# Pooled attention and a gated token MLP on one core: earlier weights, another opening order, the rank count out of PSUM, dense work on banks by turns

## The chip, the cores and the metric

The kernel runs on one core of a Trainium2 chip. Five engines run side by side, each with its own queue of instructions in order: TensorE (PE) multiplies matrices into the accumulation memory PSUM, VectorE (DVE) and ScalarE (ACT) work on SBUF and PSUM, GpSimd (POOL) on SBUF, and SyncE (SP) issues transfers to 16 DMA engines. The metric is the device time of one execution in microseconds (us), lower is better. Before the change the median of three runs is 292.88 us (292.44 to 293.79).

## The reference, cut to what matters

```python
# attention: batch 8, heads 8, sequence 576, head width 64, pool 8
k_p = k.reshape(B, H, 72, 8, D).mean(axis=3)
v_p = v.reshape(B, H, 72, 8, D).mean(axis=3)
scores = scale * q @ k_p.T                      # 576 x 72 for each head
attn = exp(scores - max); attn /= attn.sum() + 1e-9
x = concat_heads(attn @ v_p)                    # (8, 576, 512)
# mixture of depths: for each batch b
s = x[b] @ w_gate                               # 576 scores
top = the 128 largest of s
out[b] = x[b]
out[b, top] = x[b, top] + sigmoid(s[top]) * (relu(x[b, top] @ w1) @ w2)   # w1 512x1024, w2 1024x512
```

## The kernel before, in words

One path (`direct_path`) does all of it. A second, general path runs only if a flag at the end says that a softmax sum left the range for which the first path is made; it does not run here.

**Units of work.** The queries of a batch go in three thirds of 192 (`TS * TL`); `u` counts them over the batches, 0 to 23, so batch b begins at u = 3b. A chunk `a` is 128 query rows (two tiles of 64); chunk numbers run over pairs of batches, 36 in all, and a third completes one or two of them by turns (`chunks[u]`).

**Attention.** `pool_k` adds rows of keys, `k_trans` transposes and finishes them on DVE. `pool_v` adds eight rows of values into the tile `vp` (three additions), multiplies by the gate weights `wg`, and `gate_v` reduces that product, so that the gate score comes out of the same matmul as the attention (one more column, and one for the softmax sum, filled by `eights`). `q_trans(u)` transposes the queries on DVE. `scores(u)` writes four PSUM banks (bank 0 to 3) with 32 matmuls, and ACT takes the exponential from each bank into `et`. `attend(a)` multiplies `et` by `vp` into a double bank `pA` (two of these), and `norm(a)` divides on DVE and stores.

**Selection.** `score(b)` sums the gate scores over heads. `row_bcast(b)` spreads the 576 scores along the rows of banks 0 and 1 (five columns of 128) by PE transposes, and ACT copies them to the SBUF tile `sr`. `count(b)` compares the row with each column of scores by five DVE instructions of 128 to 640 values (each pair of columns is compared once, with a mask `before` for the diagonal), which leaves partial counts and the comparisons `ge`. `one_hot(b)` sums the comparisons the other way on PE, subtracts (`rank`) and compares with `slots`, `gather(b)` turns that into the list of tokens `idx` and fetches their rows with an indirect DMA from the output tensor, issued by POOL.

**Dense work.** `x_trans` transposes the fetched rows (PE, copied by ACT into `xg`), `hidden` computes the hidden layer in parts of 3, 3 and 2 blocks, with a relu on ACT after each, `finish` the second layer in parts of 176, 176 and 160 columns; ACT scales, POOL adds, and POOL scatters the rows.

**Order.** The order on every engine is written out by hand: `at(u, slot, job)` files a job into third u and slot 0 to 7, and the main loop runs slot 0, the first chunk's `attend` and `norm`, slot 1, `scores(u + 1)`, slot 2, the second chunk, `q_trans(u + 2)`, slots 3 to 7. With w = 3(b + 1), the selection of batch b lies in thirds w to w + 2 and its dense work in w + 3 to w + 5, beside the attention of the next two batches; so from u = 6 on there is dense work in every third. Jobs filed into the same slot run in the order in which the loop over batches files them. SP issues loads and stores in the same order, and a load waits there for its buffer.

Four banks are shared by all this (`bank(i, shape)`, one buffer each); the other four are the two `pA`. The next user of a bank waits until the last one is read:

```python
p = [bank(i, [128, 2, TS * TL]) for i in range(4)]      # scores
p = bank(i, [C, len(cs), C])                            # row_bcast, i = 0 and 1
p = bank(2, [C, NC])                                    # one_hot, and gather
p = bank(0, [128, DB, cap])                             # x_trans
at(w + 3, 3, hidden, b, 0, 0)                           # hidden: banks 0, 1, 0
at(w + 4, 5, finish, b, 0, 1)                           # finish: banks 1, 2, 3
```

Of the kernel before, what the change touches and what calls it, by code (L numbers as in the profile page):

```python
# [48 lines left out]
def direct_path(ctx, tc, q, k, v, moe_w_gate, moe_w1, moe_w2, moe_capacity, out, flag):  # L49
# [67 lines left out]
    for i, t in enumerate(vraws):  # L117
        (nc.vector, nc.gpsimd)[i % 2].memset(t, 0.0)

    def load_v(b, g):  # L120
# [15 lines left out]
    nc.scalar.dma_start(out=wg.rearrange("p h d -> p (h d)"),  # L136
                        in_=bass.AP(tensor=moe_w_gate.tensor, offset=moe_w_gate.offset, ap=[[0, 128], [1, DM]]))
# [10 lines left out]
    diff = counted("diff", [C, C], [[1, C]], 0, -1)  # L148
    part = counted("part", [C, 1], [[0, 1]], 0, 1)
    steps = counted("steps", [C, C // G - 1], [[-G, C // G - 1]], -G, 1)  # L150
    numbers = counted("numbers", [C, NC - 1], [[1, NC - 1]], 0, 0)
# [6 lines left out]
    for t in kts + vps:  # L158
        nc.gpsimd.memset(t, 0.0)

    slots = counted("slots", [C, NC, cap], [[C, NC], [1, cap]], 1 - NC * C, 1)

    before = const.tile([C, NC, C], FT)
    nc.gpsimd.memset(before[:, 0 : NC - 1, :], 1.0)
# [11 lines left out]
    def constants():  # L176
        nc.vector.tensor_scalar(ident, diff, 0.0, None, op0=OP.is_equal)
        nc.vector.tensor_scalar(before[:, NC - 1, :], diff, 0.0, None, op0=OP.is_lt)
        nc.vector.memset(ones, 1.0)
        nc.vector.memset(one32, 1.0)  # L180

        ge, q16, q4, lo, hi = (const.tile([C, n], FT, name=x) for x, n in (
            ("ge", C // G - 1), ("q16", 1), ("q4", 1), ("lo", 1), ("hi", 1)))
        nc.vector.tensor_scalar(ge, steps, 0.0, None, op0=OP.is_ge, op1=OP.add, accum_out=q16)
        nc.vector.tensor_scalar(q4, q16, 4.0, None, op0=OP.mult)
        nc.vector.scalar_tensor_tensor(hi, q16, -float(G), part, op0=OP.mult, op1=OP.add)
        nc.vector.tensor_scalar(hi, hi, float(TG), None, op0=OP.mult)
        for i, a in enumerate(auxb):
            nc.vector.tensor_scalar(a[:, 0 : NC - 1, 0], numbers, 0.0, hi, op0=OP.mult, op1=OP.add)
            nc.vector.tensor_copy(a[:, NC - 1, 0:1], hi)  # L190
            nc.vector.tensor_scalar(a[:, i : i + NC - 1, 1], numbers, q4, None, op0=OP.add)
            h = (NC - 1) * (1 - i)
            nc.vector.tensor_scalar(a[:, h, 1:2], q16, float(32 - 4 * i), None, op0=OP.add)
# [35 lines left out]
    def pool_v(b, g, eng):  # L229
        x = VR[b, g]  # L230
        VP[b] = vps[b % 2]
        h = slice(HG * g, HG * g + HG)
        eng.tensor_tensor(out=x[:, :, 0:4, :], in0=x[:, :, 0:4, :], in1=x[:, :, 4:8, :], op=OP.add)  # L233
        eng.tensor_tensor(out=x[:, :, 0:2, :], in0=x[:, :, 0:2, :], in1=x[:, :, 2:4, :], op=OP.add)  # L234
        eng.tensor_tensor(out=VP[b][:, h, 0:D], in0=x[:, :, 0, :], in1=x[:, :, 1, :], op=OP.add)  # L235

        eng.tensor_tensor(out=x[:, :, 2, :], in0=VP[b][:, h, 0:D], in1=wg[:, h, :], op=OP.mult)  # L237
# [45 lines left out]
    def attend(a):  # L283
        PA[a] = psum.tile([C, 2, 512], FT, name="pA")
        for h in range(H):
            g, n = divmod(h, HG)
            for t in range(2):
                u, i = divmod(2 * a + t, TS)
                nc.tensor.matmul(PA[a][TL * t : TL * t + TL, g, E * n : E * n + E],  # L289
                                 ET[u][h // 2][:, h % 2, TL * i : TL * i + TL], VP[u // NTH][:, h, :],  # L290
                                 start=True, stop=True)
# [71 lines left out]
    def row_bcast(b):  # L363
        SR[b] = work.tile([C, NC, C], FT, name="sr", bufs=1)
        for i, cs in enumerate((range(0, NC - 1), range(NC - 1, NC))):
            p = bank(i, [C, len(cs), C])
            for c in cs:
                nc.tensor.transpose(p[:, c - cs[0], :], scs[b % 2][:, c : c + 1].to_broadcast([C, C]), ident)  # L368
            nc.scalar.copy(out=SR[b][:, cs[0] : cs[-1] + 1, :], in_=p)  # L369

    def count(b):

        CN[b] = work.tile([C, NC], FT, name="cn")
        GE[b] = [work.tile([C, c + 1, C], BF, name=f"ge{c}", bufs=1) for c in range(NC)]
        for c in range(NC):
            nc.vector.scalar_tensor_tensor(GE[b][c], SR[b][:, 0 : c + 1, :], scs[b % 2][:, c : c + 1],  # L376
                                           before[:, NC - 1 - c : NC, :], op0=OP.is_ge, op1=OP.mult,
                                           accum_out=CN[b][:, c : c + 1])

    def one_hot(b):  # L380

        p = bank(2, [C, NC])
        for c in range(NC):
            for i in range(c, NC):
                nc.tensor.matmul(p[:, c : c + 1], GE[b][i][:, c, :], ones, start=(i == c), stop=(i == NC - 1))
        rank = work.tile([C, NC, 1], FT, name="rank")
        nc.vector.tensor_tensor(out=rank[:, :, 0], in0=CN[b], in1=p, op=OP.subtract)
        OH[b] = work.tile([C, NC, cap], BF, name="oh", bufs=1)
        nc.vector.tensor_tensor(out=OH[b], in0=slots, in1=rank.to_broadcast([C, NC, cap]), op=OP.is_equal)

    def gather(b):

        p = bank(2, [cap, 5])
# [21 lines left out]
    def x_trans(b):  # L415
        p = bank(0, [128, DB, cap])
# [47 lines left out]
    for b in range(B):  # L464
        w = NTH * (b + 1)
        if b % 2:
            at(w - 1, 7, score, b)
        else:
            at(w, 1, score, b)
        for n, f in enumerate((row_bcast, count, one_hot, gather, gate, x_trans)):  # L470
            du, slot = ((0, 1), (0, 2), (0, 6), (1, 4), (1, 6), (2, 5))[n] if b == B - 1 else (
                (0, 3), (0, 7), (1, 3), (1, 7), (2, 2), (2, 7))[n]
            at(w + du, slot, f, b)
        at(w + 3, 3, hidden, b, 0, 0)
        at(w + 3, 5, hidden, b, 1, 1)
        at(w + 4, 3, hidden, b, 2, 0)
        at(w + 4, 5, finish, b, 0, 1)
        at(w + 5, 5, finish, b, 1, 2)
        at(w + 5, 6, finish, b, 2, 3)
        if b + 1 < B:  # L480
            u = NTH * b
            at(u, 1, pool_k, b + 1, nc.gpsimd)
            at(u, 7, pool_v, b + 1, 0, nc.gpsimd)
            at(u + 1, 3, k_trans, b + 1)
            at(u + 1, 7, pool_v, b + 1, 1, nc.gpsimd)
            at(u + 2, 3, gate_v, b + 1, 0)
            at(u + 2, 7, gate_v, b + 1, 1)
        if b + 2 < B:
            at(u, 2, load_k, b + 2)
            at(u, 2, load_v, b + 2, 0)  # L490
            at(u + 1, 3, load_v, b + 2, 1)
            at(u + 1, 3, load_q, b + 2)
# [9 lines left out]
    at(2, 2, lambda: nc.sync.dma_start(out=w1, in_=moe_w1.rearrange("(a p) f -> p a f", p=128)))  # L502
    at(3, 3, lambda: nc.sync.dma_start(out=w2, in_=moe_w2.rearrange("(a p) n -> p a n", p=128)))
    constants()
    pool_k(0, nc.vector)
    pool_v(0, 0, nc.gpsimd)
# [5 lines left out]
    eights()  # L512
    gate_v(0, 0)
    pool_v(0, 1, nc.vector)
    gate_v(0, 1)

    for u in range(NU + 6):
        run(u, 0)
        mine = chunks.get(u, ())
        for a in mine[0:1]:  # L520
            attend(a)
            norm(a)
        run(u, 1)
        if 0 < u < NU - 1:
            scores(u + 1)
        run(u, 2)
        for a in mine[1:]:
            attend(a)
            norm(a)
# [371 lines left out]
```

## Time and profile before

| | us | share of the span |
|---|---|---|
| span of the profiled execution | 292.5 | |
| PE busy | 222.7 | 76% |
| PE weight loads busy | 205.6 | 70% |
| DVE busy | 147.9 | 51% |
| ACT busy | 72.9 | 25% |
| POOL busy | 156.9 | 54% |
| data moved | 46.94 MB | 161 GB/s in the mean |

A busy time is a sum over stages that have different limits, so the table alone doesn't say what bounds the kernel. The page's second part cuts the span into 40 slices of 7.3 us (digits are tenths of busy time, PEclk tenths of the full TensorE clock that was granted). The largest groups are the hidden layer (PE, line 430, 64.2 us), the second layer (line 442, 59.2 us with its two widths), the attention (line 289, 46.6 us) and the scores (line 277, 43.8 us); on DVE the count (line 376, 37.8 us) and the normalisation (line 306, 22.1 us); on POOL the value pooling (lines 233 to 237). A line such as "PE bank L430 <- ACT sr L369: 5.7, 7, 1.1" among the waits says that PE, at the instruction of line 430, waited for ACT's instruction of line 369, 5.7 us in total, 7 times, at most 1.1 us. In the timeline a line begins with start and length in us, then engine, line, operation, output and input; what stands in brackets at its end is the idle time of the engine ahead of it and what ended it.

### The profile page before, as it was taken

The page shows a single profiled execution, that of the slowest core. Times are in us where ns is not written, and L with a number is a line of the kernel's source. Part 1 is how long each engine was busy: PE and PEld are TensorE (multiplying, and loading weights), DVE is VectorE, ACT ScalarE, POOL GpSimd, SP SyncE. Part 2 cuts the span into 40 slices and gives each one's busy share as a digit, 9 for nine tenths or more (in the row PEclk, how much of TensorE's full clock was granted, in tenths as well). Part 3 has the DMA queues.
Part 4 walks back from the last instruction along what each step waited for, and adds up shares of the span by engine and source line. Part 5 has one row for each costly group of instructions (what it writes and reads, how often), then busy time and mean ns, then how long its engine had stood idle before and what let it go on. Part 6 is the DMA issues. An engine that isn't in the chain of part 4 may idle for free.

```text
span 292.5 us, 7287 instructions
## 1 busy us (share of the span) xinstructions
PE 222.7 (76%) x3050; PEld 205.6 (70%) x3050; DVE 147.9 (51%) x367; ACT 72.9 (25%) x178; POOL 156.9 (54%) x191
## 2 busy tenths in 40 slices
PE   0071777174889898997898989987989899899980
PEld 0061666063789797886797878876978789799980
DVE  7978758934247166816474358443862443331000
ACT  2040225020213232332232233213222321212110
POOL 9499608665910979088906693679348102413221
PEclk9996879576879999999999999999999999999996
DMA  7998899953932567215943691312122202401001
GB/s 227 355 343 325 269 360 406 333 213 95 351 126 74 186 217 260 63 57 154 346 157 115 211 318 54 94 31 81 20 64 99 74 17 61 142 0 38 38 0 47
DMA packets 13048, 46.94 MB, mean 161 GB/s; under 512 B 1104, under 2 KB 1104, under 8 KB 10960
## 3 DMA queue, kind: packets, MB, share of 16 engines
q1 hardware_dynamic: 11584, 41.95, 42.4%
q0 software_dynamic: 1280, 4.20, 4.6%
q8 instruction: 26, 0.43, 0.6%
q10 hardware_dynamic: 144, 0.26, 0.3%
q14 instruction: 14, 0.11, 0.1%
HBM read 34.87 MB, written 11.53 MB: 159 GB/s over the span
## 4 chain that ended last, share of the span: by engine, by line
PE 50%; POOL 17%; DVE 12%; issue 10%; ACT 4%; DMA 3%; POOLq 0%; ACTq 0%
PE bank L430 16%; PE bank L442 14%; PE bank L277 8%; PE pA L289 8%; POOL vraw L233 5%; DMA vraw<-in_v_dram 3%; DVE ge L376 3%; POOL vraw L234 3%; DVE qt L267 2%; ACT et L281 2%; POOL kraw L215 2%; POOL vp L235 2%; POOL vraw L237 1%; ACT sr L369 1%; PE bank L368 1%
## 5 line engine op out<-in xcount | busy, mean ns | idle before, releaser
L430 PE MATMUL bank<-xg,w 128*128 128x128 f32 x512 | 64.2, 284 | 9.4 <-ACT sr L369 5.7
L430 PEld LDWEIGHTS bank<-xg,w 128*128 128x128 f32 x512 | 60.4, 196 | 13.5 <-ACT sr L369 7.4
L442 PE MATMUL bank<-w,ht 128*128 128x176 f32 (+1 forms) x384 | 59.2, 311 | 5.0 <-ACT et L281 5.0
L281 ACT ACTIVATE et<-bank 128x384 f32<-128x384 f32 x96 | 39.3, 496 | 92.6 <-PE bank L277 92.6
L442 PEld LDWEIGHTS bank<-w,ht 128*128 128x128 f32 x384 | 55.8, 190 | 6.3 <-ACT et L281 6.2
L444 POOL TENSOR_TENSOR y<-y,xr 128x176 f32<-128x176 f32 (+1 forms) x24 | 13.0, 543 | 85.5 <-ACT y L443 84.7
L277 PE MATMUL bank<-qt,kt 32*128 32x192 f32 x768 | 43.8, 364 | 18.3 <-DVE qt L267 14.4
L289 PE MATMUL pA<-vp,et 128*64 128x66 f32 x1152 | 46.6, 234 | 12.4 <-DVE vp L241 12.0
L289 PEld LDWEIGHTS pA<-vp,et 128*64 128x64 f32 x1152 | 40.8, 146 | 18.8 <-DVE vp L241 7.2
L376 DVE SCALAR_TENSOR_TENSOR ge<-sr,sc,before 128x128 bf16<-128x128 f32 (+4 forms) x40 | 37.8, 1003 | 30.1 <-ACT sr L369 30.1
L277 PEld LDWEIGHTS bank<-qt,kt 32*128 32x128 f32 x768 | 35.9, 205 | 20.9 <-issue 17.6
L233 POOL TENSOR_TENSOR vraw<-vraw 128x1024 f32<-128x1024 f32 x15 | 35.9, 2394 | 4.4 <-DMA vraw<-in_v_dram 4.2
L267 DVE STREAM_TRANSPOSE qt<-qraw 128x512 f32<-128x512 f32 (+1 forms) x48 | 24.5, 551 | 0.0
L432 ACT ACTIVATE ht<-bank 128x384 f32<-128x384 f32 (+1 forms) x24 | 10.9, 455 | 52.1 <-PE bank L430 52.1
L298 DVE RECIPROCAL rzall<-pA 128x8 f32<-128x8 f32 x36 | 7.3, 203 | 30.6 <-PE pA L289 30.6
L306 DVE TENSOR_TENSOR xs<-pA,rzall 128x512 f32<-128x512 f32 x32 | 22.1, 692 | 1.1
L443 ACT ACTIVATE y<-bank,g 128x176 f32<-128x176 f32 (+1 forms) x24 | 9.7, 403 | 52.3 <-PE bank L442 52.3
L413 DVE RECIPROCAL g<-g 128x1 f32<-128x1 f32 x8 | 1.3, 164 | 41.0 <-POOL g L412 41.0
L234 POOL TENSOR_TENSOR vraw<-vraw 128x512 f32<-128x512 f32 x15 | 19.4, 1290 | 1.2
L215 POOL TENSOR_TENSOR kraw<-kraw 128x1152 f32<-128x1152 f32 x7 | 18.4, 2628 | 0.0
L235 POOL TENSOR_TENSOR vp<-vraw 128x256 f32<-128x256 f32 x15 | 11.5, 767 | 1.2
L237 POOL TENSOR_TENSOR vraw<-vp,wg 128x256 f32<-128x256 f32 x15 | 11.4, 759 | 1.2
(85 smaller groups left out, 167.0 us busy)
## 6 DMA issues: line engine op xcount, KB each, us to landing
kraw<-in_k_dram SPq DMA_DIRECT2D x8, 1152.0 KB
qraw<-in_q_dram SPq DMA_DIRECT2D x8, 1152.0 KB
vraw<-in_v_dram SPq DMA_DIRECT2D x16, 512.0 KB
out_dram<-xs SPq DMA_DIRECT2D x16, 512.0 KB
w<-in_moe_w_dram SPq DMA_DIRECT2D x2, 2048.0 KB
vraw<-in_v_dram SPq DMA_DIRECT2D x16, 64.0 KB
out_dram<-xh SPq DMA_DIRECT2D x8, 128.0 KB
wg<-in_moe_w_gate_dram ACTq DMA_DIRECT2D x1, 256.0 KB
```

The source lines that it names most:

```text
L215: eng.tensor_tensor(out=x[:, :, 0:2, :], in0=x[:, :, 0:2, :], in1=x[:, :, 2:4, :], op=OP.add)
L233: eng.tensor_tensor(out=x[:, :, 0:4, :], in0=x[:, :, 0:4, :], in1=x[:, :, 4:8, :], op=OP.add)
L234: eng.tensor_tensor(out=x[:, :, 0:2, :], in0=x[:, :, 0:2, :], in1=x[:, :, 2:4, :], op=OP.add)
L235: eng.tensor_tensor(out=VP[b][:, h, 0:D], in0=x[:, :, 0, :], in1=x[:, :, 1, :], op=OP.add)
L267: nc.vector.transpose(out=QT[u][:, :, n : n + m, :].rearrange("p j t c -> p t j c"), in_=x)
L277: nc.tensor.matmul(p[i][:, s, :], KT[b][r, j, s, :], QT[u][r, j, :, G * s : G * s + G], start=(j == 0), stop=(j == 1))
L281: nc.scalar.activation(ET[u][i], p[i], AF.Exp, scale=exp_scale)
L289: nc.tensor.matmul(PA[a][TL * t : TL * t + TL, g, E * n : E * n + E], ET[u][h // 2][:, h % 2, TL * i : TL * i + TL], VP[u // NTH][:, h, :] ...
L306: nc.vector.tensor_tensor(out=XS[a][:, 0 if XS.get(a - 1) is not XS[a] else 1, :].rearrange("p (g n d) -> p g n d", g=2, d=D), in0=o[:, :, ...
L376: nc.vector.scalar_tensor_tensor(GE[b][c], SR[b][:, 0 : c + 1, :], scs[b % 2][:, c : c + 1], before[:, NC - 1 - c : NC, :], op0=OP.is_ge, ...
L430: nc.tensor.matmul(p[:, n, :], w1[:, d, 128 * f : 128 * f + 128], XG[b][:, d, :], start=(d == 0), stop=(d == DB - 1))
L442: nc.tensor.matmul(p, HT[b][:, f, :], w2[:, f, c], start=(f == 0), stop=(f == FB - 1))
```

## The change

It has seven parts. (1) The load of the first weights goes from third 2 to third 0 and that of the second from 3 to 1, ahead of batch 2's data, whose loads are filed a third later; the gate weights are loaded by SP's queue. (2) At the start, two of the four value buffers are cleared later and by POOL alone, the constants of the selection move from the head of DVE's queue to slot 3 of third 0, and `eights` comes first. (3) Where DVE pools values (one half of batch 0), a single reduction takes the place of three additions, and POOL always multiplies by the gate weights. (4) `row_bcast` leaves the row in banks 0 and 1, and `count` reads it there; its fifth comparison is split, as the row lies in two banks. `one_hot` puts the rank into PSUM. (5) The dense jobs and the selection use other banks, given by the schedule. (6) In thirds with one chunk, half of its heads are attended ahead of the next scores and half behind them. (7) The slots change: POOL's pooling of values comes ahead of the gather, the row of scores ahead of the hidden layer, the gather ahead of finish.

```diff
     vraws = [const.tile([128, HG, POOLW, D], FT, name=f"vraw{i}") for i in range(4)]
-    for i, t in enumerate(vraws):
-        (nc.vector, nc.gpsimd)[i % 2].memset(t, 0.0)
+
+    nc.vector.memset(vraws[0], 0.0)
+    nc.gpsimd.memset(vraws[1], 0.0)
...
-    for t in kts + vps:
+    for t in kts + vps + vraws[2:]:
         nc.gpsimd.memset(t, 0.0)
...
+        if eng is nc.vector:
+            eng.tensor_reduce(out=VP[b][:, h, 0:D], in_=x.rearrange("p h t d -> p h d t"), axis=AX.X, op=OP.add)
+        else:
...
-        eng.tensor_tensor(out=x[:, :, 2, :], in0=VP[b][:, h, 0:D], in1=wg[:, h, :], op=OP.mult)
+        nc.gpsimd.tensor_tensor(out=x[:, :, 2, :], in0=VP[b][:, h, 0:D], in1=wg[:, h, :], op=OP.mult)
...
     def row_bcast(b):
-        SR[b] = work.tile([C, NC, C], FT, name="sr", bufs=1)
...
-            nc.scalar.copy(out=SR[b][:, cs[0] : cs[-1] + 1, :], in_=p)
+        SR[b] = [bank(0, [C, NC - 1, C]), bank(1, [C, 1, C])]
...
         for c in range(NC):
-            nc.vector.scalar_tensor_tensor(GE[b][c], SR[b][:, 0 : c + 1, :], scs[b % 2][:, c : c + 1],
-                                           before[:, NC - 1 - c : NC, :], op0=OP.is_ge, op1=OP.mult,
-                                           accum_out=CN[b][:, c : c + 1])
...
+            if c == NC - 1:
+                nc.vector.tensor_scalar(GE[b][c][:, 0:n, :], SR[b][0], s, None, op0=OP.is_ge, op1=OP.add,
+                                        accum_out=CN[b][:, NC : NC + 1])
+            x, y, m = ((GE[b][c], SR[b][0][:, 0:n, :], before[:, NC - 1 - n :, :]) if c < NC - 1 else
+                       (GE[b][c][:, c : c + 1, :], SR[b][1], before[:, NC - 2 : NC - 1, :]))
+            nc.vector.scalar_tensor_tensor(x, y, s, m, op0=OP.is_ge, op1=OP.mult, accum_out=CN[b][:, c : c + 1])
+        nc.vector.tensor_tensor(out=CN[b][:, NC - 1 : NC], in0=CN[b][:, NC - 1 : NC], in1=CN[b][:, NC : NC + 1], op=OP.add)
...
-        for n, f in enumerate((row_bcast, count, one_hot, gather, gate, x_trans)):
-            du, slot = ((0, 1), (0, 2), (0, 6), (1, 4), (1, 6), (2, 5))[n] if b == B - 1 else (
-                (0, 3), (0, 7), (1, 3), (1, 7), (2, 2), (2, 7))[n]
-            at(w + du, slot, f, b)
-        at(w + 3, 3, hidden, b, 0, 0)
-        at(w + 3, 5, hidden, b, 1, 1)
-        at(w + 4, 3, hidden, b, 2, 0)
-        at(w + 4, 5, finish, b, 0, 1)
-        at(w + 5, 5, finish, b, 1, 2)
-        at(w + 5, 6, finish, b, 2, 3)
+        last = b == B - 1
+
+        at(*((w - 1, 3) if b % 2 else (w, 1)), score, b)
+        at(w, 1 if last else 3, row_bcast, b)
+        at(w, 1 if last else 3, count, b)
+        at(*((w, 7) if last else (w + 1, 3)), one_hot, b, 0)
+        at(w + 1, 5, gather, b, 3)
+        at(w + 2, 5, gate, b)
+        at(w + 2, 5, x_trans, b, 2)
+        at(w + 3, 4, hidden, b, 0, 2)
+        at(w + 3, 6, hidden, b, 1, 3)
+        at(w + 4, 4, hidden, b, 2, 1)
+        at(w + 4, 6, finish, b, 0, 2)
+        at(w + 5, 4, finish, b, 1, 0)
+        at(w + 5, 6, finish, b, 2, 1)
         if b + 1 < B:
             u = NTH * b
-            at(u, 1, pool_k, b + 1, nc.gpsimd)
-            at(u, 7, pool_v, b + 1, 0, nc.gpsimd)
+            at(u, 2, pool_k, b + 1, nc.gpsimd)
+            at(u, 5, pool_v, b + 1, 0, nc.gpsimd)
+            at(u + 1, 2, pool_v, b + 1, 1, nc.gpsimd)
             at(u + 1, 3, k_trans, b + 1)
-            at(u + 1, 7, pool_v, b + 1, 1, nc.gpsimd)
-            at(u + 2, 3, gate_v, b + 1, 0)
-            at(u + 2, 7, gate_v, b + 1, 1)
+            at(u + 2, 2, gate_v, b + 1, 0)
+            at(u + 2, 3, gate_v, b + 1, 1)
         if b + 2 < B:
-            at(u, 2, load_k, b + 2)
-            at(u, 2, load_v, b + 2, 0)
+            at(u + 1, 2, load_k, b + 2)
+            at(u + 1, 2, load_v, b + 2, 0)
             at(u + 1, 3, load_v, b + 2, 1)
-            at(u + 1, 3, load_q, b + 2)
+            at(u + 2, 2, load_q, b + 2)
...
-    at(2, 2, lambda: nc.sync.dma_start(out=w1, in_=moe_w1.rearrange("(a p) f -> p a f", p=128)))
-    at(3, 3, lambda: nc.sync.dma_start(out=w2, in_=moe_w2.rearrange("(a p) n -> p a n", p=128)))
-    constants()
+    at(0, 2, lambda: nc.sync.dma_start(out=w1, in_=moe_w1.rearrange("(a p) f -> p a f", p=128)))
+    at(1, 0, lambda: nc.sync.dma_start(out=w2, in_=moe_w2.rearrange("(a p) n -> p a n", p=128)))
+    eights()
...
+    at(0, 3, constants)
...
-        for a in mine[0:1]:
-            attend(a)
-            norm(a)
+        if len(mine) == 1:
+            attend(mine[0], range(HG))
+        elif mine:
+            attend(mine[0])
+            norm(mine[0])
         run(u, 1)
         if 0 < u < NU - 1:
             scores(u + 1)
+        if len(mine) == 1:
+            attend(mine[0], range(HG, H))
         run(u, 2)
```

## The prediction, made before the changed kernel was run

> **What bounds the kernel now.** I read the page's second part first (the span in 40 slices): TensorE (PE) is nearly full from slice 11 on and ragged before, with its clock granted at 0.6 to 0.9 where it is ragged. So I asked for busy time by stretches, and split the span at 70.5 us, where the seventh third of a batch (u = 6) begins, the first whose dense work runs.
>
> ```profile
> 0.00:10.00 10.00, 0.00 (x0) 0.00 (x0) 8.20 (x21) 1.49 (x2) 7.90 (x21) 1.00 0.79 274
> 10.00:20.00 10.00, 5.45 (x64) 4.61 (x64) 8.27 (x15) 1.71 (x5) 7.00 (x5) 1.00 1.05 343
> 20.00:30.00 10.00, 2.94 (x56) 2.67 (x56) 8.58 (x8) 1.57 (x4) 9.68 (x7) 0.71 0.86 308
> ...
> 40.00:50.00 10.00, 8.83 (x177) 7.14 (x173) 5.68 (x16) 4.59 (x12) 5.28 (x8) 0.94 1.01 387
> 50.00:60.00 10.00, 2.67 (x46) 2.31 (x47) 9.90 (x15) 1.07 (x3) 5.83 (x4) 0.58 0.89 322
> ...
> 100.00:130.00 30.00, 27.62 (x402) 25.55 (x402) 16.74 (x40) 8.91 (x22) 19.81 (x23) 1.00 0.52 171
> ```
>
> After the stretch and its length come PE, PE weight loads, VectorE (DVE), ScalarE (ACT) and GpSimd (POOL) in busy us, then clock, DMA share and GB/s. From 100 us PE works 27.6 of 30 us and nobody else is near full. Before 70.5 us it works 31 us, while DVE (up to 9.9 of 10), POOL and the DMA take turns to hold it up. Two problems, then. Next the waits of PE, first from 70.4 us on, then two lines of the stretch before it:
>
> ```profile
> PE bank L430 <- ACT sr L369: 5.7, 7, 1.1
> PE bank L442 <- ACT et L281: 5.0, 5, 1.4
> PE pA L289 <- DVE vp L241: 5.0, 5, 1.9
> PE bank L430 <- ACT et L281: 3.7, 6, 0.6
> PE bank L368 <- ACT ht L432: 3.5, 6, 0.6
> PE bank L368 <- ACT xg L420: 0.7, 1, 0.7
> ...
> PE pA L289 <- DVE vp L241: 7.1, 1, 7.1
> PE bank L418 <- DMA xr<-out_dram,idx: 4.3, 1, 4.3
> ```
>
> The first six add up to 23.6 us; 1.9 of it is the entry to u = 6 itself, so 21.7 us lie inside the PE-bound part. All but 5.0 are waits for a PSUM bank that ACT still reads, not for data. Last, the timeline of the opening:
>
> ```profile
> 18.40 3.29 DVE L233 TENSOR_TENSOR vraw<-vraw 128x1024 f32<-128x1024 f32 x1
> ...
> 27.88 2.91 PE L289 MATMUL pA<-vp,et 128*64 128x66 f32 x48 [7.06 <-DVE vp L241]
> ...
> 49.89 2.69 DVE L376 SCALAR_TENSOR_TENSOR ge<-sr,sc,before 128x384 bf16<-128x384 f32 x1
> ...
> 61.38 1.20 POOL L403 DMA_INDIRECT xr<-out_dram,idx  x1 [0.71 <-DMA vraw<-in_v_dram]
> 62.62 2.37 POOL L233 TENSOR_TENSOR vraw<-vraw 128x1024 f32<-128x1024 f32 x1
> ...
> 68.03 0.63 PE L418 MATMUL bank<-ident,xr 128*128 128x128 f32 x4 [4.26 <-DMA xr<-out_dram,idx]
> ...
> 70.59 2.03 PE L289 MATMUL pA<-vp,et 128*64 128x66 f32 x32 [1.93 <-DVE vp L241]
> ```
>
> DVE pools the second half of batch 0's values slowly (9.4 us in all, to 27.8); the first count is slow (2.69 us for one of its five); and POOL, in order, stands at batch 0's gather until 61.4 with the last value pooling of batch 2 behind it, so u = 6 starts at 70.6.
>
> [...] the 128x384 count takes 2.69 us at 49.9 us beside POOL and 0.61 at 82.0 us with POOL idle; the value sum takes 3.29 us. [...] a reader holds its bank; the first, second, fourth, fifth and sixth waits above are that.
>
> **The change, part by part.**
> *Start.* The first constants leave DVE's head: they held it from 5.06 to 8.63 us. In their place stand the eights, 1.9 us by their rows (0.46, 0.14, 0.23, 2 x 0.55), which can start at about 5 us (POOL from 0.72: one fill of 1.80 instead of two, keys 0.37, four fills of 0.53). So key pooling starts near 6.7 instead of 8.6 and scores(0) near 12 instead of 14.
> *Pooling of the second half on DVE.* Three additions and a product, 3.29 + 1.77 + 2.45 + 1.37 = 8.9 us, become one reduction. The nearest row, 512 values in 0.69 us, gives 0.15 + 2048 x 1.04 ns = 2.3 us[...]. The product goes to POOL (0.69), behind the first half's pooling there, which ends at 18.1 (it began at 12.77, on data, and that stays). The gate follows at about 19.3 instead of 27.8: 8.5 us.
> *Constants at (0, 3).* They now stand behind q_trans(2) on DVE: 3.5 to 6 us as they meet POOL; norms of u = 1 queue behind them. DVE from 19.3: four norms at 1.05, three query transposes at 1.03, constants 5, key transpose 2.1, gates 0.8, about 15, so 34. POOL: product to 18.9, batch 1 keys 4.0 and values 2 x 5.1, so 33. u = 3 starts near 34 (before: 40.8).
> *Weights ahead of batch 2.* The two batches and the gate are 7.34 MB, in by 24 us (2.74 + 3.43 MB at 20). Then 4.2 MB of weights, a store and keys, 5.9 MB at 0.35 MB/us (between 343 and 387 GB/s): keys of batch 2 near 41, values 44, queries 48. They came earlier before, but POOL is only free at 33, so it waits some 7 us here: what the opening gives back. Pooling of batch 2: 41 + 4 + 10 = 55.
> *Count from PSUM.* The copies (0.75 us on ACT) go. The row is read from PSUM[...]: undisturbed 0.35 + 0.48 + 0.61 + 0.75, then 0.65 and 0.35 for the split fifth, a sum of 0.15[...]: 3.7 us (mean before 5 x 1.003 + reads; first 7.9). The new hold: banks 0 and 1 until the count ends. scores(u+1) queue on PE for them, with everything after. In steady state the count starts 2.0 us after the attention (norm 1.0, transposes 1.0) and ends at 5.7; PE has 0.7 + 5.9 of row and hidden work and half an attention (0.55), 7.1 us. Hidden by that, with 1.4 us to spare.
> *POOL order.* The last value pooling of batch 2 is ahead of gather(0) and ends at 55; the gather's index follows at once, its rows land 3.6 to 6.5 us after issue (the trace's extremes are 3.3 and 6.5), 59 to 62; x_trans(0), then u = 6. Entry to u = 6: 60.5 instead of 70.6, a gain of 10 us (6 to 14 by bus rate and landing).
> *Banks by turns, split attention.* Hidden goes to banks 2, 3, 1 and finish to 2, 0, 1, so nobody waits for the row's copy (5.7), for a hidden part's eviction (3.5) or xg (0.7). Behind the scores stand 0.55 us of half an attention where there was nothing, and ACT needs 0.5 us for the first bank and about 0.4 for each next: 5.0 + 3.7 falls to about 1. The order of value pooling and gates takes 3.1 (5.0 less the entry). Removed: 21.7 - 1 = 20.7.
> *New wait.* gather now comes right after hidden part 2, ahead of finish. Behind the attention DVE has norm 1.0, transposes 1.0, rank 0.16, one-hot 0.83 + 0.07: ready at 3.1. PE gets there after 0.4 + 2.0 = 2.4. So 0.7 us of PE, with finish and the next third queued behind, six times: 4.2 (0 if DVE is early, 9 if it is 1.5 each). Its consumer, x_trans, comes 8 us after the gather matmul and index, issue and landing need 2 + 1.3 + 3.6, so that stays hidden. Net steady gain 20.7 - 4.2 = 16.5.
> Start-up of the last batch and the 8.5 us after the last dense matmul (284 to 292.5) stay as they are.
>
> **The rivals.**
> Forecast: 292.9 - 10 - 16.5 = 266.4, both gains. For it: the waits are named, and each has its bank or its queue in the code. Chance 0.56.
> *The data of batch 2 is the bound.* DMA runs at 0.86 to 1.05 of its engines before 60 us already; if the weights' 12 us push batch 2 so far that u = 6 begins at 70 again, only the steady gain is left: 276.4. Against: the slices near 30 us show the bus half empty, as SyncE waited for buffers. 0.16.
> *Banks held by the count or late gathers eat the steady gain.* DVE is used 16.7 of 30 us and each of its delays now reaches PE twice. Only the opening is left: 283. 0.09.
> *Better.* PE ends with few waits: 222.7 us of busy PE, some at a low clock, and an opening at 57: 257. 0.12.
> *Slower.* The count keeps its disturbed length (7.9) in PSUM and scores stand 3 us more per batch, the gather wait is 1.5 us, and batch 2 is late: 292.9 + 7 x 3 + 9 - 20.7 + 0 = 302; a milder mix ends near 296. [...] 0.07.
>
> **How the numbers follow.** Likeliest is 266.4. From 257 to 280 the range takes in the forecast with its bounds, the better case, the late batch 2, and leaves out half of the bank case and the slower one. Faster: 0.56 + 0.16 + 0.09 + 0.12 = 0.93; of the slower case's 0.07 I give 0.01 to no change and 0.06 to slower.
>
> **What would show it.** Right: PE's waits after u = 6 for the row's copy and for the hidden eviction gone, a new one for the one-hot near 0.7 us; thirds of a batch, three together, near 27.6 us where they took 30.3 (first finish parts at 121.58 and 242.60 us in the chain, four batches apart); the first gated attention near 19 us, u = 3 near 34 and u = 6 near 60; count instructions under 1 us even beside POOL. Wrong: scores waiting for DVE's count; x_trans waiting for the gathered rows in every batch; POOL waiting on the bus past 45 us; u = 6 near 70.

## The result, and the profile after

The changed kernel takes 272.94 us in the median of four runs (268.81 to 274.07), the kernel before 293.34 beside it; the ratio is 0.9225, with a 95% interval of 0.9107 to 0.9343. Ratios here and below leave out executions more than 1.5% above the fastest of the same kernel, here 274.07 and 273.46, so that 0.9225 stands for 270.61 us. The forecast was 266.4, in a range of 257 to 280. So the direction and the size were right, but not their make-up: of the 26.5 us forecast, 10 were to come from the opening and 16.5 from the rest. The profiled executions (292.5 and 270.6 us) say that the opening gave nothing and the rest 22.6.

First the busy times by stretches, cut where u = 6, the first third with dense work, starts its attention (70.59 us before, 71.31 after). The columns are those of the prediction. The kernel before:

```profile
70.59:292.50 221.91, 191.78 (x2509) 179.04 (x2509) 95.64 (x262) 58.52 (x144) 110.80 (x138) 0.97 0.37 118
```

and after:

```profile
0.00:71.31 71.31, 35.17 (x541) 30.95 (x542) 46.48 (x107) 13.07 (x31) 52.95 (x63) 0.80 0.89 324
71.31:270.60 199.29, 188.14 (x2510) 176.40 (x2509) 91.10 (x280) 53.42 (x131) 102.19 (x131) 0.97 0.38 120
```

Length less PE's busy time is PE's idle time: 30.1 us before, 11.2 after, so 19.0 less; 3.6 us of busy time went as well. PE's waits after 71.31 us have shrunk to one line, where six stood before:

```profile
PE bank L405 <- DVE oh L397: 3.0, 5, 0.6
```

It is the new wait that was forecast, for the one-hot list (L405 is `gather`). The waits ahead of 71.31 us:

```profile
PE bank L281 <- DVE qt L271: 11.7, 2, 11.2
PE bank L428 <- DMA xr<-out_dram,idx: 9.2, 1, 9.2
PE pA L294 <- DVE rzall L303: 4.7, 1, 4.7
PE bank L281 <- DVE ge L382: 3.5, 1, 3.5
PE bank L281 <- DVE kt L228: 2.6, 1, 2.6
PE bank L405 <- DVE oh L397: 2.5, 1, 2.5
```

The first is the start. The second is where the opening was lost: PE stands at `x_trans(0)` (L428) for 9.2 us, and the next attention, in order behind it, begins with u = 6. The timeline of the opening, POOL and PE mixed, shows what it stood for:

```profile
13.07 3.69 DVE L235 TENSOR_REDUCE vp<-vraw 128x256 f32<-128x2048 f32 x1 [1.09 <-DMA vraw<-in_v_dram]
...
42.46 0.20 POOL L362 CAST auxb<-sc 128x5 bf16<-128x5 f32 x1 [10.41 <-DVE sc L355]
...
58.21 0.25 POOL L409 TENSOR_SCALAR idx<-tok 128x1 int32<-128x1 f32 x1
...
61.92 1.21 POOL L413 DMA_INDIRECT xr<-out_dram,idx  x1 [3.46 <-issue]
...
70.29 1.09 PE L428 MATMUL bank<-ident,xr 128*128 128x128 f32 x4 [9.21 <-DMA xr<-out_dram,idx]
71.31 1.15 PE L294 MATMUL pA<-vp,et 128*64 128x66 f32 x16
```

POOL is done with the gather's index at 58.46 us (58.21 + 0.25) but issues the gather at 61.92. In the 3.46 us between it waits for nothing that the profile shows ("issue"). Then the rows take 8.2 us to land, that is, from the issue until they are in SBUF. PE's clock is low all the while: the slices from 54 to 74 us (the 9th to 11th) read 5, 6 and 5 tenths, and right behind the wait, from 71.3 to 76 us, the granted clock is 0.50.

```profile
PE   0396176680699999999999999999999999999970
...
PEclk9999669656589999999999999999999999999995
```

### The profile page after: what moved, and what is told of

It is laid out like the page before. It is cut to its first block, busy times and chain, and to the rows that moved or that the text cites. A ratio compares the mean times of both kernels' runs of the same rounds, so it can differ in the third digit from the quotient of the medians.

```text
span 270.6 us, 7289 instructions
## 1 busy us (share of the span) xinstructions
PE 223.3 (83%) x3050; PEld 207.3 (77%) x3050; DVE 137.6 (51%) x387; ACT 66.5 (25%) x162; POOL 155.1 (57%) x193
## 4 chain that ended last, share of the span: by engine, by line
PE 69%; DVE 13%; DMA 8%; issue 4%; POOL 3%; ACT 0%; POOLq 0%; DVEq 0%
PE bank L452 21%; PE bank L440 18%; PE bank L281 14%; PE pA L294 13%; DMA out_dram<-xs 5%; DVE qt L271 3%; DMA xr<-out_dram,idx 3%; DVE oh L397 2%; PE bank L371 2%; PE bank L428 2%; DVE xs L311 1%; DVE auxb L192 1%; DVE vp L203 1%; PE bank L405 1%; DVE ge L386 1%
## 5 line engine op out<-in xcount | busy, mean ns | idle before, releaser
L281 PE MATMUL bank<-qt,kt 32*128 32x192 f32 x768 | 46.6, 380 | 18.3 <-DVE qt L271 11.7
L440 PE MATMUL bank<-xg,w 128*128 128x128 f32 x512 | 60.5, 277 | 0.0
L440 PEld LDWEIGHTS bank<-xg,w 128*128 128x128 f32 x512 | 58.4, 192 | 0.5 <-ACT et L285 0.5
L294 PEld LDWEIGHTS pA<-vp,et 128*64 128x64 f32 x1152 | 42.4, 152 | 15.7 <-issue 14.9
L281 PEld LDWEIGHTS bank<-qt,kt 32*128 32x128 f32 x768 | 38.6, 216 | 20.6 <-POOL sc L168 11.2
L294 PE MATMUL pA<-vp,et 128*64 128x66 f32 x1152 | 49.0, 241 | 6.1 <-DVE rzall L303 4.7
L409 POOL TENSOR_SCALAR idx<-tok 128x1 int32<-128x1 f32 x8 | 1.9, 244 | 31.6 <-DVE g L411 31.4
L386 DVE SCALAR_TENSOR_TENSOR ge<-bank,sc,before 128x128 bf16<-128x128 f32 (+3 forms) x40 | 18.2, 498 | 1.6 <-PE bank L371 1.6
L362 POOL CAST auxb<-sc 128x5 bf16<-128x5 f32 x8 | 1.6, 202 | 21.1 <-DVE sc L358 10.7
L428 PE MATMUL bank<-ident,xr 128*128 128x128 f32 x32 | 5.3, 292 | 9.2 <-DMA xr<-out_dram,idx 9.2
```

The costliest lines, as they stand in the source:

```text
L281: nc.tensor.matmul(p[i][:, s, :], KT[b][r, j, s, :], QT[u][r, j, :, G * s : G * s + G], start=(j == 0), stop=(j == 1))
L386: nc.vector.scalar_tensor_tensor(x, y, s, m, op0=OP.is_ge, op1=OP.mult, accum_out=CN[b][:, c : c + 1])
L440: nc.tensor.matmul(p[:, n, :], w1[:, d, 128 * f : 128 * f + 128], XG[b][:, d, :], start=(d == 0), stop=(d == DB - 1))
```

## The experiments

All are edits of the changed kernel, run beside the kernel before; ratios are to that, with 95% intervals. A gain or loss in us beside a ratio is its difference from the changed kernel's 0.9225, at 293.34 us. The changed kernel's interval overlaps those of seven of the twelve runs, so there the traces must say what a gain is made of. A useful mark beside the time is the start of the first whole hidden block (48 matmuls of L440), 77.09 us in the changed kernel. Theory A is that the opening's gain is lost where PE stands, in order, for the gathered rows; its DMA form puts the late rows down to data queued ahead of them. Theory B: batch 2's own data come late, as the weights go first. C: the constants on DVE hold up the opening. D: the first store does. F, formed later: POOL's own instructions are fetched late.

**x_trans of batch 0 moved to where it is used.**

```diff
-        at(w + 2, 5, x_trans, b, 2)
+        at(*((w + 2, 5) if b else (w + 3, 3)), x_trans, b, 2)
```

> Batch 0's x_trans moves from third 5 to third 6, behind the row of scores' slot and ahead of the hidden layer. Theory A (the opening's gain is lost at PE's in-order wait for batch 0's gathered rows): the 9.2 us wait shrinks to 3 or less, u = 6 starts near 64 instead of 71, the dense work near 72 instead of 77: about 267 us, ratio 0.91 to 0.905. Theory B (batch 2's own data come late because the weights go first): attend of u = 6 finds its data no earlier, time unchanged near 272.

265.38 us median (262.79 to 272.33, six runs), ratio 0.8947 (0.8851 to 0.9043): 8.2 us. The profiled execution is the longest of the six, as long as the changed kernel; in it the gather is issued 5.3 us after its index, lands in 9.9, and PE still waits 7.6 us for the rows, a third of a batch later. Moving x_trans doesn't make the rows any earlier. The gain of the shorter executions fits A, that PE's place in order is most of the loss, but no trace shows one of these, so this kernel alone doesn't prove it.

**Batch 4's loads a third later**, away from the gather.

```diff
-            at(u + 1, 2, load_k, b + 2)
+            d = int(b == 2)
+            at(u + 1 + d, 2, load_k, b + 2)
```

(and the two loads of values likewise)

> Only batch 4's keys and values are issued one third later; batch 0's gathered rows no longer share the DMA with them. Theory A in its DMA form: issue to landing of the first gather falls from 8.2 us to 4 to 5, the PE wait from 9.2 to 5 or 6, time near 269. If the rows are late for another reason (the 3.5 us before the issue, or stores of batch 0), landing stays near 8 and the time near 272. Theory B: unchanged.

274.05 us, ratio 0.9308 (0.9225 to 0.9392), no gain:

```profile
63.82 1.21 POOL L413 DMA_INDIRECT xr<-out_dram,idx  x1 [5.47 <-DMA qraw<-in_q_dram]
70.76 1.09 PE L428 MATMUL bank<-ident,xr 128*128 128x128 f32 x4 [8.37 <-DMA xr<-out_dram,idx]
```

The rows land in 6.8 us instead of 8.2 (4 to 5 was expected), but the gather is issued 5.5 us late. The loads of batch 4 are not the cause, and A in this form falls.

**The weights back to thirds 2 and 3.**

```diff
-    at(0, 2, lambda: nc.sync.dma_start(out=w1, in_=moe_w1.rearrange("(a p) f -> p a f", p=128)))
-    at(1, 0, lambda: nc.sync.dma_start(out=w2, in_=moe_w2.rearrange("(a p) n -> p a n", p=128)))
+    at(2, 2, lambda: nc.sync.dma_start(out=w1, in_=moe_w1.rearrange("(a p) f -> p a f", p=128)))
+    at(3, 3, lambda: nc.sync.dma_start(out=w2, in_=moe_w2.rearrange("(a p) n -> p a n", p=128)))
```

> The two weight loads go back to thirds 2 and 3, all else as in the changed kernel. Theory A: the weights' place is worth nothing by itself, POOL stood at batch 0's score and not at batch 2's keys, 270 to 275. Theory B (weights ahead cost the opening): faster by the late batch 2, about 266. If the weights ahead are themselves what made the kernel faster: 278 or more, with the hidden layer waiting for them.

270.57 us, ratio 0.9207 (0.9128 to 0.9285): the same as the changed kernel, and B falls. Whether the weights go ahead of batch 2 or not is worth nothing that this can tell; the rows were waited for 5.0 us here.

**The constants of the selection two thirds later.**

```diff
-    at(0, 3, constants)
+    at(2, 1, constants)
```

> The constants move from third 0 to third 2, where DVE sat idle 3.9 us. Theory C (DVE's 6.5 us of constants in front of the norms of u = 1 hold up the opening): attend of u = 2 no longer waits 4.7 us, u = 3 starts near 34 instead of 40, and if this reaches u = 6 the time is near 266 to 268. Theory A: u = 3 starts earlier but the gathered rows are still what u = 6 waits for; the gain is what the gather's issue comes forward, 0 to 4 us: 268 to 273.

266.59 us, ratio 0.9059 (0.8982 to 0.9136): 4.9 us. PE waits 1.2 us for rzall instead of 4.7, and the rows are waited for 2.6. A new wait appears, on DVE:

```profile
44.60 0.69 DVE L311 TENSOR_TENSOR xs<-pA,rzall 128x512 f32<-128x512 f32 x1 [5.84 <-DMA out_dram<-xs]
```

The first store, issued at 28.82 us, took 15.70 us to land, and its buffer is one of two. The count stands behind that, and scores(5) behind the count (9.2 us, 3.5 in the changed kernel). So the index comes no earlier than in the changed kernel (58.21):

```profile
58.24 0.25 POOL L409 TENSOR_SCALAR idx<-tok 128x1 int32<-128x1 f32 x1 [5.31 <-DVE g L411]
59.19 1.20 POOL L413 DMA_INDIRECT xr<-out_dram,idx  x1 [0.71 <-POOL idx L409]
```

What came forward is the gather's issue (2.7 us) and, with a landing of 5.7 us, the rows (5.3). That is the kind of gain that A expects, though the time is the one that C named.

**The same, with three store buffers.**

```diff
-            XS[a] = work.tile([C, 2, DM], FT, name="xs")
+            XS[a] = work.tile([C, 2, DM], FT, name="xs", bufs=3)
```

> Constants in third 2 as before, and a third buffer for the normalised rows xs. With the constants moved DVE stood 5.8 us at the store of the first rows, which landed 15.7 us after its issue behind 4.2 MB of weights and batch 2. Theory D (the slow first store is the next thing that holds the opening): that wait is gone, count(0) starts near 40 instead of 46, and the gather comes up to 6 us earlier: 261 to 264. If the gather itself must wait for the same stores, or POOL for batch 2, the time stays near 266.

265.99 us, ratio 0.9063 (0.8994 to 0.9131), no better than with two:

```profile
53.20 0.25 POOL L409 TENSOR_SCALAR idx<-tok 128x1 int32<-128x1 f32 x1
55.95 1.21 POOL L413 DMA_INDIRECT xr<-out_dram,idx  x1 [2.50 <-DMA qraw<-in_q_dram]
63.44 1.09 PE L428 MATMUL bank<-ident,xr 128*128 128x128 f32 x4 [6.57 <-DMA xr<-out_dram,idx]
```

The store wait is gone and the index is 5 us earlier than in the changed kernel, but from the index to the rows' first use it takes 10.2 us, where with two buffers (58.24 to 64.99) it took 6.8.

**Constants later and weights back.** Both edits above (without the third buffer).

> Constants in third 2, and the weight loads back in thirds 2 and 3, two buffers for xs. Theory D: the first store no longer queues behind the weights, lands within 6 us, DVE doesn't stand at it: 261 to 265. If the weights' place is worth nothing here either: 266 to 267. If the hidden layer or batch 3 now waits: over 268.

265.34 us, ratio 0.9036 (0.8969 to 0.9103): as constants alone. DVE's wait for the store is gone, as D says, and the index comes at 52.59, but the gather's issue is again 2.7 us late and the rows land 7.9 us after it, so this isn't the weights' traffic either.

**Sixteen idle fills on POOL.** In six kernels the trace has one 8 KB transfer on an instruction queue (q14), called the fetch here, just ahead of the late gather, always by the same distance, 2.0 to 2.2 us from its start (1.7 to 1.9 from its end, as each takes 0.31 us); a seventh, with the attention not split, shows it too:

```
kernel                       fetch starts   gather issued
changed                      59.81          61.92
x_trans moved                62.27          64.30
batch 4's loads later        61.79          63.82
weights back                 59.37          61.48
constants later, 3 buffers   53.82          55.95
constants later, weights     53.42          55.58
attention not split          58.35          60.40
```

In three of these the profile names a load of queries as what ended POOL's idle time, as in two of the lines above; the fixed distance speaks against it. In the kernel with the constants later alone the fetch (53.87) fell in POOL's idle time, and the gather (59.19) followed its index at once. Theory F takes these transfers for POOL's next instructions, fetched late, through the same busy bus (0.82 of the DMA engines from 54 to 60 us in the changed kernel). If so, fills that POOL runs while idle near 32 us move its instruction stream on, and the fetch falls there.

```diff
+    def filler():
+        for i in range(16):
+            nc.gpsimd.memset(fill[:, i : i + 1], 0.0)
+
+    at(2, 5, filler)
```

> The changed kernel with sixteen one-column fills on POOL in third 2, where POOL waits 10 us anyway; nothing else differs. Theory F (the 3.5 us in which the gather wasn't issued, 58.5 to 61.9 us, are an instruction fetch queued behind the data, since an 8 KB fetch is seen 1.8 us ahead of the gather): the fetch falls into POOL's idle time, the gather follows its index by under 1 us, PE's wait for the rows falls from 9.2 to 5 or 6, time near 269. If the gather waits for batch 3's queries or for a store: unchanged, 272 to 273.

267.03 us, ratio 0.9076 (0.9007 to 0.9145): 4.4 us from 16 instructions that do nothing. POOL's and PE's timeline:

```profile
57.85 0.25 POOL L409 TENSOR_SCALAR idx<-tok 128x1 int32<-128x1 f32 x1
58.80 1.21 POOL L413 DMA_INDIRECT xr<-out_dram,idx  x1 [0.71 <-DMA vraw<-in_v_dram]
...
64.91 1.08 PE L428 MATMUL bank<-ident,xr 128*128 128x128 f32 x4 [2.81 <-DMA xr<-out_dram,idx]
```

The index is 0.36 us earlier than in the changed kernel, the gather 3.1, the rows 5.4. The changed kernel has an instruction transfer at 36.98 us and the next at 59.81; with the fills they start at 35.12 and 37.01, and the views up to 67 us show no other. The view of the queues for the microsecond from 59 us on in the changed kernel,

```profile
q1 hardware_dynamic: 32, 0.21, 49.2%
q14 instruction: 1, 0.01, 1.9%
```

and here from 35 us on, where the changed kernel has none (packets, MB, share of the engines):

```profile
q1 hardware_dynamic: 112, 0.38, 96.6%
q14 instruction: 1, 0.01, 1.9%
```

So with no fetch ahead of the gather the issue follows the index 2.8 us sooner (0.95 us for 3.71, start to start), as theory F expects; that these are POOL's instructions, and that the busy bus makes them late, is argued, not shown. The landing got shorter with it (6.0 for 8.2 us), of which this kernel doesn't give the cause.

**The row copied to SBUF, as before**, and counted there; the rest as changed.

```diff
+        sr = work.tile([C, NC, C], FT, name="sr", bufs=1)
+        nc.scalar.copy(out=sr[:, 0 : NC - 1, :], in_=SR[b][0])
+        nc.scalar.copy(out=sr[:, NC - 1 : NC, :], in_=SR[b][1])
+        SR[b] = [sr[:, 0 : NC - 1, :], sr[:, NC - 1 : NC, :]]
```

> ACT copies the row of scores from banks 0 and 1 to SBUF and the count, still split, reads it there. If the PSUM read keeps the count clear of POOL: its instructions go from 0.50 us in the mean to 0.8 or more, the first count from 2.9 us to 5 or more; PE's wait at the next scores in the opening goes (the banks come free after the copy) but the one-hot comes later; steady thirds unchanged, time 272 to 276. If reading PSUM is what holds banks and costs time: 268 to 271.

275.63 us, ratio 0.9403 (0.9311 to 0.9495), 5.2 us slower. The count's groups by shape in this kernel,

```profile
L390 DVE SCALAR_TENSOR_TENSOR ge<-sr,sc,before 128x384 bf16<-128x384 f32 x8 | 14.6, 1831 | 0.0
L390 DVE SCALAR_TENSOR_TENSOR ge<-sr,sc,before 128x512 bf16<-128x512 f32 x8 | 12.5, 1564 | 0.0
...
L386 DVE TENSOR_SCALAR_CACHE_REDUCE ge<-sr,sc 128x512 bf16<-128x512 f32 x8 | 5.9, 737 | 0.0
```

stand against 611 and 744 ns from PSUM. The last group reads one SBUF tile and no mask, and keeps its 737 ns. The first count takes 9.4 us (2.9). In it, beside POOL's pooling of values, 128x256 took 2.56 us and 128x384 1.60, where in the changed kernel, beside POOL's pooling of keys, they took 0.48 and 0.61. After u = 6 PE's waits for the one-hot list come to 6.6 us (3.0), for the count to 0.8 (0), and from the first whole hidden block to the end it takes 198.4 us against 193.5, so the steady thirds do change, which was not expected. With POOL idle, the kernel before did 128x384 from SBUF in 0.61 us (at 81.99 us). So what the runs show slowed beside POOL is the comparison with row and mask both in SBUF (1831 ns in the mean), and not the one with a single SBUF input (737; 0.73 us at 53.45 us, beside POOL). Most of the cost is the longer count, not the copy: PE nowhere waits for the copy, and the longer waits for DVE, 4.4 us, are nearly the whole 4.9.

**The attention not split.**

```diff
-            attend(mine[0], range(HG))
+            attend(mine[0])
...
-        if len(mine) == 1:
-            attend(mine[0], range(HG, H))
```

> Undoes one part: in thirds with one chunk the whole attention stands ahead of the next scores again. Theory (half of it behind the scores is what PE does while ACT takes the exponentials; before, PE waited 8.7 us in all for ACT et after u = 6): some 0.6 us or more come back at each of the 10 to 11 such thirds, so 279 to 284, and waits of PE for ACT et of 5 to 9 us appear. Rival (the split only moves the same work, and the bank order alone removed these waits): 273, no such waits. Rival B: the whole attention ahead gives the count less time, so the scores wait for DVE ge: waits of L281 <- DVE ge grow instead.

269.41 us, ratio 0.9146 (0.9074 to 0.9218): not slower, so the size in the theory falls. PE's waits after 60 us:

```profile
PE bank L428 <- DMA xr<-out_dram,idx: 4.8, 1, 4.8
PE bank L405 <- DVE oh L397: 1.9, 3, 0.6
PE bank L371 <- ACT et L285: 1.9, 3, 0.6
PE bank L452 <- ACT et L285: 1.9, 3, 0.6
PE bank L394 <- ACT et L285: 1.9, 3, 0.6
```

The waits for the exponentials do come back, 5.7 us, but the attention is 1.3 us shorter over four batches and the list is waited for less. From the first whole hidden block to the end it takes 195.9 us (71.76 to 267.7) against 193.5 in the changed kernel (77.09 to 270.6): the split is worth 2.4 us. What hides that is the opening: the index is 1.8 us earlier, and the first gather landed in 4.5 us instead of 8.2.

**The banks of before**, with the row held in banks 0 and 1 by the count.

```diff
-        at(w + 3, 4, hidden, b, 0, 2)
-        at(w + 3, 6, hidden, b, 1, 3)
-        at(w + 4, 4, hidden, b, 2, 1)
+        at(w + 3, 4, hidden, b, 0, 0)
+        at(w + 3, 6, hidden, b, 1, 1)
+        at(w + 4, 4, hidden, b, 2, 0)
```

(finish 1, 2, 3; one_hot and gather 2; x_trans 0)

> The dense jobs and the selection on the banks of before (hidden 0, 1, 0; finish 1, 2, 3; one_hot and gather 2; x_trans 0), with the row still held in banks 0 and 1 by the count and everything else as in the kernel after. Theory (banks by turns are what makes the count in PSUM harmless): hidden part 0 behind the row waits for the count, 3 to 4 us in every batch with count and dense work together (6), and hidden parts wait for their own eviction (3.5 us before): 290 to 300. Rival (other jobs were the reason; PE is done with what it can do meanwhile in another third): under 277.

312.14 us, ratio 1.0616 (1.0519 to 1.0713): slower than the kernel before, and by more than either theory said.

```profile
PE bank L440 <- DVE ge L382: 22.7, 6, 4.1
...
PE bank L440 <- issue: 3.9, 1, 3.9
PE bank L394 <- ACT et L285: 3.1, 6, 0.7
PE bank L452 <- ACT et L285: 2.8, 5, 0.7
```

The hidden layer waits for the count to leave bank 0, near 4 us in each of six batches (for the first the profile names no releaser, "issue") and 2.7 in a seventh, and after the long waits it runs slowly:

```profile
110.57 7.23 PE L440 MATMUL bank<-xg,w 128*128 128x128 f32 x48 [3.98 <-DVE ge L382]
...
269.92 5.60 PE L440 MATMUL bank<-xg,w 128*128 128x128 f32 x48 [2.72 <-DVE ge L382]
```

The block of the changed kernel that the first of these stands against:

```profile
104.29 5.52 PE L440 MATMUL bank<-xg,w 128*128 128x128 f32 x48
```

PE's clock was lower: over 100 to 130 us 0.94 was granted, where the changed kernel had 1.00, and single matmuls of the hidden layer took up to 550 ns, 275 in the median. So the block behind 3.98 us of waiting took 1.71 us more, and the one behind 2.72 us next to nothing more (5.60 for 5.52). A batch takes 33.09 us ((209.14 - 76.77) / 4) against 26.84 ((184.46 - 77.09) / 4): 3.99 of waiting, 1.61 in slower hidden blocks, and most of the rest for the exponentials.

**Three moves together**: x_trans of batch 0 beside its hidden layer, constants later with three store buffers, and the fills.

> x_trans of batch 0 beside its hidden layer, constants a third later with three store tiles, and 16 one-column fills on POOL ahead of the first gather's instructions. Theory (what is left of the loss is PE standing in order at the fetched rows; the earlier opening then reaches u = 6): the entry to u = 6 near 60 us, no wait there for xr over 1 us, and 257 to 261 in all. Rival (the opening is bound elsewhere, by the data of batch 2 or by DVE, and the single moves share one gain): 263 to 266, as with either alone.

260.38 us (258.81 to 261.69), ratio 0.8824 (0.8735 to 0.8913). The first whole hidden block starts at 65.90, 11.2 us earlier than in the changed kernel, and the kernel is 11.8 us faster. Alone they brought 8.2, 4.8 and 4.4, or 17.4: they share a gain, as the rows' wait can be cured only once. After 60 us PE's waits are

```profile
PE bank L405 <- DVE oh L397: 3.0, 5, 0.6
PE bank L281 <- DVE qt L271: 1.7, 1, 1.7
PE bank L428 <- ACT et L285: 0.7, 1, 0.7
PE bank L428 <- DMA xr<-out_dram,idx: 0.2, 1, 0.2
```

**The same, with the gather behind finish.**

```diff
-        at(w + 1, 5, gather, b, 3)
+        at(w + 1, 5 if last else 7, gather, b, 3)
```

> The same, and the gather of every batch but the last behind the finish part (slot 7) instead of ahead of it, so that DVE has 3 us more for the one-hot list. Theory: the five or six waits of PE for DVE oh, 3.0 us, vanish, and the rows still land in time for x_trans, a third later: 254 to 258, 3 us under the joint kernel. Rival (the gather, issued 3 us later and slow to land, now ends after x_trans is reached): waits of PE for DMA xr of about 1 us or more in each batch, time the same as the joint kernel or longer.

256.47 us (256.12 to 256.87), ratio 0.8705 (0.8636 to 0.8774), the best of all and 15.3 us faster than the changed kernel. The 3.0 us are gone; instead PE waits for the rows twice:

```profile
PE bank L428 <- DMA xr<-out_dram,idx: 1.6, 2, 0.9
PE bank L428 <- ACT g L421: 0.7, 1, 0.7
```

A batch takes 26.33 us ((169.00 - 63.70) / 4). Of the 4.9 us between the profiled executions (259.9 and 255.0) only 2.7 lie behind the start of the first whole hidden block; the other 2.2 are there before the edit can act, as the first row of scores already stands at 39.87 us for 41.35. So the edit is worth some 2.7 us.

## Why the prediction was right, and where it was wrong

The total came out within the range, but luck has a part in it: the opening gave nothing where 10 us were forecast, and the steady part 6.1 us more than its share.

**The step that failed** is "Entry to u = 6: 60.5 instead of 70.6, a gain of 10 us". It was 71.3, outside the 6 to 14 that it allowed for. Up to the gather the opening runs much as laid out, 3.2 us late:

| | predicted | measured |
|---|---|---|
| scores(0) | near 12 | 11.2 |
| reduction on DVE | 2.3 | 3.7 |
| first gated attention | 19.3 | 18.7 |
| constants | 5 (3.5 to 6) | 6.6 (22.63 to 29.2) |
| attention of u = 3 | 34 | 36.9 |
| first count, with its closing sum | 3.7 | 4.3 (banks free after 2.9) |
| POOL done with batch 2 | 55 | 58.2 |
| index to gather issue, start to start | at once | 3.7 |
| gather landing | 3.6 | 8.2 |

The last three make up 10.6 of the 10.8 us: 3.2 from POOL being late, 2.8 from the issue (3.7 for an ordinary 0.95, as with the fills) and 4.6 from the landing. POOL did wait in the middle, but 10.4 us and not for the bus: for batch 0's score (L362 <- L355), so for the attention, which was late behind the norms, which stood in DVE's queue behind the constants. The term "POOL waits some 7 us here: what the opening gives back" had the wrong releaser, and the trace of the kernel before had shown the right one:

```profile
44.35 0.20 POOL L357 CAST auxb<-sc 128x5 bf16<-128x5 f32 x1 [10.39 <-DVE sc L350]
```

Moving the constants brought the score 5.3 us forward (36.98 for 42.24), and POOL was done with batch 2 at 52.9. The index came forward by 5 us only with the third store buffer or with the weights back as well, and issue and landing then took most of that back. The constants alone and the fills left the index where it was (58.24 and 57.85): what they won at the rows, 5.3 and 5.4 us, is issue and landing.

The issue was given no time, as POOL would be free. It was free, but the issue stood until 2.1 us after the start of an instruction transfer (59.81 and 61.92 us); without one ahead of it, in the kernel with the fills, it took 0.95 us. The landing was taken from the middle of the trace, 3.6, though this gather is the one that falls into a busy stretch of the bus (0.79 of the DMA engines while the rows were under way in the changed kernel): the 6.5 that the prediction gives as the trace's extreme was this very one, and it took 4.5 to 9.9 us over the twelve kernels that count in PSUM. The prediction named "x_trans waiting for the gathered rows" as a sign against it, but for every batch; it came in one, and cost 9.2 us.

**The rival "the data of batch 2 is the bound"** gives the right entry (70) for another reason. Batch 2's data were there: POOL pooled without a pause from 43.69 to 58.2, and with the weights elsewhere nothing changed.

**The steady gain** was under-sized: 16.5 for 22.6. No wait of before is left (21.7 us gone, where 20.7 were counted), the new one came five times instead of six and at 0.6 us each: 3.0 for 4.2. Most of the rest, 3.6 us, is PE's busy time, which the forecast left as it was. The hidden layer alone took 64.2 us in the kernel before and 60.5 here: 1.6 of it is one block of batch 0 that ran at a granted clock of 0.63 there (4.57 us for 24 matmuls, elsewhere 2.94); the other 2.2 come of two such blocks, 5.9 us together when something stood between them, that are now one of 48 in 5.5. A batch takes 26.84 us, where 27.6 was forecast.

**The count** is as forecast or better in its comparisons: 611 ns for 128x384 beside POOL, 2.69 us before. That a row in PSUM would keep it so was the author's estimate, which no trace of before showed; with the row in SBUF it took 1831 ns. Of the 3.7 us forecast, the six comparisons and the sum, priced from the trace of before, add up to 3.3; the rest was not shown. Its closing sum, one value from two SBUF inputs, was priced at 0.15 us and took 0.16 to 1.61; it holds no bank. Reading PSUM hardly cost more: the comparison with one input took 745 ns from PSUM and 737 from SBUF (with the row copied), the one with two inputs 744 against 0.75 with POOL idle. The banks that the count holds did no harm in the steady part, as 1.4 us to spare said; in the opening, scores(5) stood 3.5 us for them.

**Banks by turns and split attention** were priced together. Apart, the split is worth 2.4 us, and the banks are worth far more than the waits they were priced by, since the count in PSUM makes them needed: without them the kernel is some 41 us slower. The rival "banks held by the count" was therefore a real danger, and the bank order is what kept it off.

**Not settled:** why the first gather lands in anything between 4.5 and 9.9 us. Taking away batch 4's loads or moving the weights didn't bring it under 6.8. Nor is it shown why the instruction transfer comes when it does.

## What to carry to other kernels

When work is moved forward, ask of the last link ahead of the bound engine (here a gather and the transposes that stand in order for it) what it costs at the new time and under that load, and put the waiting instruction beside its consumer. A resource that a faster operation now holds longer, such as a bank, must be priced together with whoever uses it next: the count in PSUM and the order of banks are one edit. Behind a wait of PE near 4 us the matmuls took another 1.3 to 2.3 us here (with the banks of before), behind one of 2.7 us next to nothing.

## What the hardware showed that was not expected

- POOL stood idle for 3.5 us between index and gather in the changed kernel, with no wait in the trace, and for 1.7 to 5.5 us in others, three times with a load of queries named for it. In seven kernels an 8 KB instruction transfer began 2.0 to 2.2 us ahead of the gather's issue. With 16 one-column fills there was none ahead of it, the idle time was 0.71 us, and the profiled execution was 5.0 us shorter (270.6 and 265.6 us).
- The first store landed 14.0 us after its issue in the changed kernel and 15.7 with the constants later, in a stretch where the DMA engines were busy (0.92 of them in the first 60 us).
- A reduction over the middle of a tile (2048 values to 256, on DVE) took 3.69 us, 1.73 ns per value beyond the 0.15 us of a short instruction (7 values, L185), where one of 512 to 256, 0.69 us, had shown 1.04. It ran beside POOL, so the runs don't say how much of it is the layout.
- Four values per partition took DVE 2.32 us beside POOL (L192, 26.83 to 29.15 us); the same instruction had taken 0.22 us just before. The slow one ended with POOL's addition (26.79 to 29.13), and so did the closing sum of the first count (1.42 us, to 50.12; POOL to 50.10).
